# Clamps of weight words moved to VectorE, the causal mask of the maxima to TensorE, and new ranks in a planned attention and expert kernel

## The chip, the cores and the metric

The kernel runs on one core of one Trainium2 chip. Its engines work at the same time, each through its own queue of instructions in order: TensorE (PE; PEld is its weight load), VectorE (DVE), ScalarE (ACT), GpSimd (POOL), and SyncE (SP), which issues the DMAs. They wait for each other by semaphores. The metric is the device time of one execution in microseconds, lower is better.

## The reference

Inputs are float32 except where the weights come as float64, read as pairs of 32-bit words. Four batches, 8 heads, 576 positions, 64 columns a head:

```python
scores = scale * np.matmul(q, k.transpose(0, 1, 3, 2))
log_f = np.log(np.clip(f, 0.0001, 1.0))
cum = np.cumsum(log_f, axis=-1)
scores = np.where(causal, -1e9, scores + cum[:, :, :, None] - cum[:, :, None, :])
attn = softmax(scores)                 # with its row maximum subtracted
x = (attn @ v), heads side by side     # 2304 tokens x 512
x = (x @ w_a) * (x @ w_b) @ w_out      # 512 -> 1536 -> 512
h = x @ w_in                           # 512 -> 1024
solu = h * softmax(h)
out = layernorm(solu) * g_ln @ w_out2  # 1024 -> 512
```

## The kernel before

Products are made of parts: a float32 operand is split into a rounded high part (ScalarE casts it to the matmul's format) and the rest (a subtraction on VectorE or GpSimd), and three products high by high, low by high, high by low are added in PSUM.

**The stages.** Attention goes head by head. The first batch's heads are done twice, for their first 256 queries (kind K0) and for the rest (K1); those of the other three batches in one piece (KF). Per head: `turn` transposes k and q (line 752), `split_k` and `split_q` split them (763 to 784), `max_scores` multiplies once (806), takes each row's maximum with the causal mask added (819), transposes the maxima (828) and writes them as extra rows of q (840, 845); `scores` multiplies again with the maxima in (863 to 871), `exps` applies the exponential and splits it (913 to 937), `weigh` multiplies by v (969), `out_` divides (991 to 1023). `split_x` splits the result (1041 to 1046), and `up_unit` makes the up products (1059, 12 matmuls for w_a and 12 for w_b), multiplies the two (1080) and writes the result to DRAM (1084). There are 8 strips of tokens by 12 column tiles of such units. `down` reads it back and splits it (1292 to 1304) and makes the down products (1310, 12 matmuls a tile); `expert` does the second layer by tiles of 128 tokens: 1363, the softmax and norm (1378 to 1416), transposes (1425) and 1440.

**Weights.** `load_cols` turns a tile of doubles into float32 words: a DMA (592), then on ScalarE the high word's absolute value as a number (607) and three bits of the low word (611), a clamp to the range of exponents (616), two shifts and ors on VectorE (618, 622), for the last matrix a scale (627), ScalarE's cast (635) and the subtraction for the low part (640). There are 48 tiles of 512 columns and 8 of 256, so 56 clamps; 28 tiles are w_a and w_b, which the up products need.

**What sets the order.** Nothing is ordered by hand. Each operation is recorded with an engine (or several, the cheapest in the plan is taken), a rank `key`, a planned cost (`t_dve`, `t_pool1` and so on) and the parts of buffers it reads and writes. `Sched.run` then plays the operations through: on each engine, among those that can start within `WIN` of the first, the lowest rank goes first. Instructions are written out in that order, so a number in the table `Y` (ranks of the stages and weights, and choices) changes every queue. `fill` puts small bf16 products (1480), whose result nobody reads, on TensorE where the plan shows a gap of over 0.3 us before its 210 us; they keep TensorE busy and are real instructions in its queue.

Clamp and choice of engine, before:

```python
cl_ = op([("DVE", t_dve2(n)), ("POOL", t_pool1(n))][:Y["CL"]], key, None, ...)
cl_.fn = lambda: ENG[cl_.eng].tensor_scalar(
    out=wmv(), in0=wmv(), scalar1=W_MIN, scalar2=W_MAX, op0=ALU.max, op1=ALU.min)
```

With `CL` 2 the plan could choose, and put all 56 on GpSimd, whose planned cost was 0.67 us for 512 columns.

Of the kernel before, what the change touches and what calls it, by code (L numbers as in the profile page):

```python
# [276 lines left out]


Y = {
    "Z0": 10.901,  # L280
    "T0": 3.049,
    "T1": 5.81,
    "TA": 4.561,
    "TF": 20.444,
    "U0": 0.0,
    "U1": 1.931,
    "UF": 5.673,
    "UL": 5.395,
    "LEAD": (3.6808465587643813, 2.8668250590211586),
    "SHRINK": 0.372,  # L290
    "W0": 26.546,
    "WD0": 4.133,
    "WN": 4,
    "WD1": 0.984,
    "WD2": 2.48,
    "EZ": 15.392,
    "EO": 6.479,
    "TE": 15.456,
    "DL": 1,
    "BIAS": 0.302,  # L300
    "UO": (7.298276837196878, 10.587551391559384, 11.3464056171286),
    "UD": 48.049,
    "UK": 77.199,
    "L3": 6,
    "CL": 2,
    "TL": (0.0, 0.0),
    "F1": 210.0,
    "FG": 0.3,
    "FF": 0.7,
    "RA": 1,  # L310
    "MX": -2.229,
    "XK": -0.243,
    "WIN": 0.067,
}


# [1212 lines left out]
```

## Time and profile before

| | before |
|---|---|
| median of 3 runs | 976.86 us (975.46 to 980.66) |
| the profiled execution, its own time | 974.57 us |
| its span, first to last instruction | 972.8 us |
| TensorE busy | 930.5 us (96%), granted clock 0.988 |
| VectorE busy | 614.9 us (63%) |
| ScalarE busy | 462.5 us (48%) |
| GpSimd busy | 226.2 us (23%) |

The span is cut into stages below. The granted clock is a share of 2.4 GHz. "L616 POOL" in a row is line 616 on GpSimd; "out<-in" are the program's names of tiles (`wms`, `pfw`, `raws`, `xrw`, `nat` are buffers in which tiles are staged, `ps` is PSUM, `sets` the split k and q), and "<-ACT wms L607" is what ended the idle time before.

### The profile page before, as it was taken

Reading aid. Unit: us, or ns where it says so; the run is one execution under the profiler, and the core shown is the slowest. Engines: PE = TensorE matmul, PEld = TensorE weight load, DVE = VectorE, ACT = ScalarE, POOL = GpSimd, SP = SyncE. Lnnn points to the kernel's source line nnn. Section 1 sums busy time; section 2 is a strip of 40 time slices with the busy share of each in tenths; the row PEclk is TensorE's granted clock in tenths of the full one; section 3 lists DMA queues with packets and bytes.
Section 4 is the critical chain, followed back from the end, with each engine's and each line's share of the span. In section 5 each row is a group of like instructions: output and inputs, shape, how many; then the busy total and the mean of one; then the engine's idle time right before and its main releaser. Section 6 shows DMA issues by size and latency. Waiting matters only on the chain.

```text
span 972.8 us, 16051 instructions
## 1 busy us (share of the span) xinstructions
PE 930.5 (96%) x5878; PEld 842.9 (87%) x5878; DVE 614.9 (63%) x1207; ACT 462.5 (48%) x860; POOL 226.2 (23%) x277
## 2 busy tenths in 40 slices
PE   7888888899999999999999999999999999999997
PEld 5777877899999999999999987988888888888886
DVE  6787787777666767777663676644455554455554
ACT  4777666665664464655543564422232232232332
POOL 3265544334420220212232653300000000000000
PEclk9799999999999999999999999999999999999999
DMA  3655445333342332332334654411221212111000
GB/s 83 170 139 162 143 132 142 87 82 86 85 101 63 77 82 60 98 78 57 97 97 161 192 183 139 156 41 55 65 55 44 62 47 64 35 38 44 17 22 32
DMA packets 124002, 86.90 MB, mean 89 GB/s; under 512 B 74346, under 2 KB 114292, under 8 KB 123924
## 3 DMA queue, kind: packets, MB, share of 16 engines
q1 hardware_dynamic: 123924, 85.88, 31.7%
q8 instruction: 46, 0.75, 0.3%
q14 instruction: 32, 0.26, 0.1%
HBM read 56.86 MB, written 19.02 MB: 78 GB/s over the span
## 4 chain that ended last, share of the span: by engine, by line
PE 76%; DVE 7%; POOL 6%; ACT 5%; issue 3%; DMA 3%; SPq 1%; DVEq 0%; ACTq 0%; POOLq 0%
PE ps L1059 25%; PE ps L1310 14%; PE ps L1363 10%; PE ps L1440 9%; PE ps L969 7%; PE ps L871 3%; POOL pfw L616 2%; PE ps L806 2%; PE ps L863 2%; POOL wms L616 2%; PE ps L1425 2%; PE ps L752 1%; DVE wms L618 1%; DMA pfw<-in_moe_w_b_dram 1%; DVE wms L622 1%
## 5 line engine op out<-in xcount | busy, mean ns | idle before, releaser
L1059 PE MATMUL ps<-xs,wt 128*128 128x288 f32 (+2 forms) x2304 | 334.2, 299 | 4.9 <-DVE wt L640 3.8
L1059 PEld LDWEIGHTS ps<-xs,wt 128*128 128x128 f32 x2304 | 314.3, 189 | 8.8 <-DVE wt L640 5.0
L969 PE MATMUL ps<-pexp,VS 128*128 128x64 f32 (+5 forms) x600 | 98.4, 308 | 6.1 <-DVE pexp L935 3.5
L969 PEld LDWEIGHTS ps<-pexp,VS 128*128 128x128 f32 x600 | 93.4, 196 | 10.5 <-DVE pexp L935 4.3
L819 DVE CUSTOM_DVE_ANT_0 ps<-ps,cmask 64x576 f32<-64x576 f32 (+4 forms) x160 | 86.4, 551 | 20.0 <-PE ps L806 16.0
L1440 PE MATMUL ps<-wt 128*128 128x512 f32 x408 | 97.9, 389 | 0.0
L1310 PE MATMUL ps<-wt,sets 128*128 128x512 f32 (+1 forms) x420 | 95.3, 375 | 2.5 <-DVE wt L1302 2.5
L1440 PEld LDWEIGHTS ps<-wt 128*128 128x128 f32 x408 | 76.6, 188 | 15.9
L1310 PEld LDWEIGHTS ps<-wt,sets 128*128 128x128 f32 x420 | 73.2, 190 | 17.0 <-DVE wt L1302 4.3
L1078 ACT COPY ats<-ps 128x288 f32<-128x288 f32 (+2 forms) x96 | 38.0, 396 | 95.8 <-PE ps L1059 95.0
L922 POOL TENSOR_SCALAR_AFFINE_SELECT pfw<-pfw 128x128 f32<-128x128 f32 (+1 forms) x120 | 37.1, 338 | 185.7 <-ACT pfw L913 184.6
L1302 POOL TENSOR_TENSOR wt<-nat,wt 128x256 fp32r<-128x256 f32 (+1 forms) x9 | 8.9, 985 | 285.6 <-ACT wt L1298 285.6
L616 POOL TENSOR_SCALAR wms<-wms 128x512 f32<-128x512 f32 (+1 forms) x32 | 57.4, 1794 | 73.0 <-ACT wms L607 72.9
L1298 ACT CAST wt<-nat 128x512 fp32r<-128x512 f32 (+1 forms) x60 | 34.7, 578 | 83.4 <-PE ps L1310 74.1
L1302 DVE TENSOR_TENSOR wt<-nat,wt 128x512 fp32r<-128x512 f32 (+1 forms) x51 | 34.1, 668 | 61.6 <-ACT wt L1298 31.1
L1080 DVE TENSOR_TENSOR gts<-ps,ats 128x288 f32<-128x288 f32 (+2 forms) x84 | 38.1, 454 | 44.1 <-PE ps L1059 21.8
L1363 PE MATMUL ps<-wt 128*128 128x512 f32 x240 | 59.0, 395 | 0.7 <-DVE wt L1323 0.7
L616 POOL TENSOR_SCALAR pfw<-pfw 128x512 f32<-128x512 f32 x24 | 48.2, 2008 | 32.6 <-ACT pfw L607 32.5
L913 ACT ACTIVATE pfw<-ps 128x960 f32<-128x960 f32 (+1 forms) x48 | 38.6, 836 | 33.6 <-PE ps L871 33.4
L1363 PEld LDWEIGHTS ps<-wt 128*128 128x128 f32 x240 | 44.1, 188 | 9.8 <-DVE wt L1323 1.2
L863 PE MATMUL ps<-sets 128*128 128x64 f32 (+5 forms) x200 | 50.8, 299 | 1.8 <-DVE sets L840 1.0
L871 PE MATMUL ps<-sets 71*128 71x448 f32 (+4 forms) x200 | 51.9, 336 | 0.2
(158 smaller groups left out, 1506.4 us busy)
## 6 DMA issues: line engine op xcount, KB each, us to landing
gs<-gts SPq DMA_DIRECT2D x60, 144.0 KB
sets<-sets SPq DMA_DIRECT2D x56, 144.0 KB
nat<-gs SPq DMA_DIRECT2D x36, 144.0 KB
raws<-in_moe_w_a_dram SPq DMA_DIRECT2D x10, 512.0 KB
pfw<-in_moe_w_b_dram SPq DMA_DIRECT2D x10, 512.0 KB
nat<-gs SPq DMA_DIRECT2D x36, 128.0 KB
out_dram<-xrw SPq DMA_DIRECT2D x18, 256.0 KB
nat<-in_k_dram SPq DMA_DIRECT2D x32, 128.0 KB
```

The source lines that it names most:

```text
L616: cl_.fn = lambda: ENG[cl_.eng].tensor_scalar(out=wmv(), in0=wmv(), scalar1=W_MIN, scalar2=W_MAX, op0=ALU.max, op1=ALU.min)
L819: nc.vector.tensor_tensor_reduce(out=x, in0=x, in1=cmask[:n, off:off + w], scale=1.0, scalar=-3.0e38, op0=ALU.add, op1=ALU.max, accum_out= ...
L863: nc.tensor.matmul(dst, lhsT=SA(st)[:, ks], rhs=MA(st)[:, q0:q1], start=True, stop=False)
L871: nc.tensor.matmul(dst, lhsT=SB(st)[:D + NA, ks], rhs=MB(st)[:D + NA, q0:q1], start=False, stop=True)
L913: op(("ACT", t_act(n, True)), key + 5.5 + 0.9 * i, lambda i=i, n=n, pf=pf: nc.scalar.activation(out=pf(), in_=bank(ss[i], 0, n), func=AF.Exp),
L969: nc.tensor.matmul(bank(u, K.uo + q0, q1 - q0), lhsT=V[:, vp], rhs=src[:, o:o + q1 - q0], start=(k_ in K.first and ip == 0), stop=(k_ in K ...
L1059: nc.tensor.matmul(bank(u[m], 0, n_), lhsT=wv(m, wp, c)[:, kk], rhs=xsv(h, xx, n_)[:, kk], start=(n == 0), stop=(n == 3 * KD - 1))
L1080: op(("DVE", t_dve(n_)), key - 50.0, lambda: nc.vector.tensor_tensor(out=gtv(), in0=bank(u[1], 0, n_), in1=atv(), op=ALU.mult), r=[(u[1], ...
L1302: o.fn = lambda o=o, gr=gr, gb=gb: ENG[o.eng].tensor_tensor(out=ghv(gb, 1)[:, :n], in0=grv(gr)[:, :n], in1=ghv(gb, 0)[:, :n].bitcast(F32), ...
L1310: nc.tensor.matmul(bank(py, 512 * d, n), lhsT=WO[c][0][:, wp * DM:(wp + 1) * DM][:, ds_], rhs=ghv(gb, gp)[:, :n], start=(c == 0 and i == 0 ...
L1363: nc.tensor.matmul(bank(ph, half * 512, 512), lhsT=yv(yb, yp)[:, d, tsl], rhs=wi(d, wp)[:, fs], start=(n == 0), stop=(n == 3 * KD - 1))
L1440: nc.tensor.matmul(bank(po, 0, DM), lhsT=zp[:, c], rhs=w2(c, wp), start=(c == 0 and i == 0), stop=(c == NF2 - 1 and i == 2))
```

## The change

`CL` becomes 1: the clamp has only VectorE to choose. `MM` is new: for the first batch's heads (K0 and K1) `max_scores` adds the causal mask by a small product (identity by mask, 128 columns or 64) into the same bank of PSUM, and the maximum is a plain reduction instead of the custom add-and-maximum with its separate read of the accumulator. `TB` is new and 1, which leaves the three bits on ScalarE, as before. Three planned costs change (two of ScalarE's by 1.1, GpSimd's clamp, which is not chosen now). All other numbers of `Y` that change are ranks and the plan's weights. Lines behind the table stand a little lower in the new kernel: 616 becomes 627, 618 becomes 629, 640 becomes 651, 806 becomes 820, 819 becomes 839, 1059 becomes 1082, 1310 becomes 1333, 1480 becomes 1503; the mask's products are line 824.

```diff
-    "Z0": 10.901,
-    "T0": 3.049,
-    "T1": 5.81,
+    "Z0": 17.056,
+    "T0": 4.873,
+    "T1": 15.735,
...
-    "W0": 26.546,
-    "WD0": 4.133,
+    "W0": 0.0,
+    "WD0": 0.382,
...
-    "UD": 48.049,
-    "UK": 77.199,
+    "UD": 22.8,
+    "UK": 87.852,
     "L3": 6,
-    "CL": 2,
+    "CL": 1,
...
+    "TB": 1,
+    "MM": 1,
...
-        op(("ACT", t_act(n)), key - 0.6, lambda: nc.scalar.activation(
+        op(("ACT", t_act(1.1 * n)), key - 0.6, lambda: nc.scalar.activation(
...
-        cl_ = op([("DVE", t_dve2(n)), ("POOL", t_pool1(n))][:Y["CL"]], key, None, r=[(wm, 0)],
+        cl_ = op([("DVE", t_dve2(n)), ("POOL", 0.18 + n * 0.0034)][:Y["CL"]], key, None, r=[(wm, 0)],
...
             for o, w, i, k0 in K.mm[part]:
+                d0 = o + i * P - k0
+                dw = min(P, o + w - d0)
+                pm = K.pm and Y["MM"] and o <= d0 < o + w
                 nc.tensor.matmul(
                     bank(ms[part], o, w), lhsT=MB(st)[:D + 2, i * P:(i + 1) * P],
-                    rhs=SB(st)[:D + 2, k0:k0 + w], start=True, stop=True)
+                    rhs=SB(st)[:D + 2, k0:k0 + w], start=True, stop=not pm)
+                if pm:
+                    nc.tensor.matmul(
+                        bank(ms[part], d0, dw), lhsT=identb, rhs=cmask[:, 4 * P:4 * P + dw],
+                        start=False, stop=True)
...
+            if K.pm and Y["MM"]:
+                nc.vector.tensor_reduce(
+                    out=mt(st)[:n, 2 + i:3 + i], in_=x, op=ALU.max, axis=AX.X)
+                return
```

**VectorE in the first batch, a weight tile.** Before, between the last maxima of K0's heads and a K1 head's exponentials, the two word operations of one tile (618, 622) stand with no clamp; it is in GpSimd's queue.

```order
L1022 TENSOR_TENSOR xrw<-xrw 128x256
L618 SCALAR_TENSOR_TENSOR pfw<-pfw,raws 128x512
L935 TENSOR_TENSOR pexp<-ps,pexp 128x832
L1002 COPY xrw<-ps 64x256
L819 ISA ps,mts<-ps,cmask 64x576
L819 ISA mts 64x1
L622 SCALAR_TENSOR_TENSOR pfw<-raws,pfw 128x512
```

Now:

```order
L627 TENSOR_SCALAR wms<-wms 128x512
L1025 COPY xrw<-ps 64x256
L629 SCALAR_TENSOR_TENSOR wms<-wms,pfw 128x512
L977 TENSOR_TENSOR VS<-nat,VS 128x5x2x64
L633 SCALAR_TENSOR_TENSOR wms<-pfw,wms 128x512
L627 TENSOR_SCALAR pfw<-pfw 128x512
L839 TENSOR_REDUCE mts<-ps 128x1
L958 TENSOR_TENSOR pexp<-ps,pexp 128x832
L958 TENSOR_TENSOR pexp<-ps,pexp 128x384
L629 SCALAR_TENSOR_TENSOR pfw<-pfw,raws 128x512
```

The clamp (627) of each tile now stands in VectorE's own queue ahead of its word operations, and a maximum (839) is one instruction where it was two (819).

**TensorE around its last filler.** Before, the last filler (1480) is followed by the maxima and scores of the second batch's heads, and a head's products by v (969) lie ahead of it.

```order
L871 MATMUL ps<-sets 128x448
L1480 LDWEIGHTS identb
L1480 MATMUL ps<-cmask,identb 128x192
L1480 LDWEIGHTS identb
L1480 MATMUL ps<-cmask,identb 128x192
L1480 LDWEIGHTS identb
L1480 MATMUL ps<-cmask,identb 128x192
L806 MATMUL ps<-sets 128x512
L806 MATMUL ps<-sets 128x384
L806 MATMUL ps<-sets 128x128
L806 MATMUL ps<-sets 128x256 x2
L806 MATMUL ps<-sets 128x320
```

Now:

```order
L1503 LDWEIGHTS identb
L1503 MATMUL ps<-cmask,identb 128x192
L992 MATMUL ps<-pexp,VS 128x448 x6
L992 MATMUL ps<-pexp,VS 128x64 x3
L820 MATMUL ps<-sets 128x512
L820 MATMUL ps<-sets 128x384
L820 MATMUL ps<-sets 128x128
L992 MATMUL ps<-pexp,VS 128x320 x3
L992 MATMUL ps<-pexp,VS 128x192 x3
L992 MATMUL ps<-pexp,VS 128x128 x3
```

That head's 18 products by v now come behind the last filler. In all there are 406 fillers before and 376 now.

**TensorE at the start of the down products.** Before, behind the last head's products by v:

```order
L969 MATMUL ps<-pexp,VS 128x128 x3
L1059 MATMUL ps<-xs,wt 128x288 x492
L1310 MATMUL ps<-wt,sets 128x512 x12
L1059 MATMUL ps<-xs,wt 128x288 x24
L1310 MATMUL ps<-wt,sets 128x512 x12
```

Now:

```order
L992 MATMUL ps<-pexp,VS 128x128 x3
L1082 MATMUL ps<-xs,wt 128x288 x312
L1333 MATMUL ps<-wt,sets 128x512 x12
L1082 MATMUL ps<-xs,wt 128x288 x12
L1333 MATMUL ps<-wt,sets 128x512 x12
```

The first down product moves from behind 41 groups of 12 up products to behind 26; 69 groups in all stand behind the last head before, and 65 now.

## Rows read from the trace of the kernel before

**Rows 1.** View by stage; per engine busy us (instructions), then clock, DMA share, GB/s.
```profile
core 0: us, PE busy (x) PEld busy (x) DVE busy (x) ACT busy (x) POOL busy (x), PEclk, DMA share, GB/s
0.00:189.80 189.80, 157.10 (x1197) 139.62 (x1197) 145.48 (x302) 126.23 (x265) 87.09 (x98) 0.95 0.52 135
189.80:520.00 330.20, 329.18 (x2360) 321.46 (x2359) 226.39 (x457) 177.88 (x289) 79.58 (x145) 1.00 0.30 80
520.00:560.00 40.00, 40.00 (x294) 39.48 (x293) 23.90 (x38) 21.32 (x43) 21.27 (x12) 1.00 0.65 208
560.00:600.00 40.00, 37.47 (x195) 31.75 (x194) 29.64 (x46) 24.89 (x45) 20.75 (x11) 0.96 0.57 176
920.00:972.80 52.80, 47.54 (x234) 38.93 (x232) 27.33 (x61) 14.05 (x31) 0.54 (x1) 1.00 0.07 25
```

**Rows 2.** Groups by line on TensorE: busy us, mean ns; last, line 1480's own view.
```profile
L1059 PE MATMUL ps<-xs,wt 128*128 128x288 f32 (+2 forms) x2304 | 334.2, 299 | 4.9 <-DVE wt L640 3.8 <-DVE gts L1080 0.7 <-ACT ats L1078 0.4
...
L969 PE MATMUL ps<-pexp,VS 128*128 128x64 f32 (+5 forms) x600 | 98.4, 308 | 6.1 <-DVE pexp L935 3.5 <-DVE sets L768 2.2 <-POOL VS L954 0.3
...
L1480 PE MATMUL ps<-cmask,identb 128*128 128x192 bf16 x406 | 47.4, 264 | 0.6 <-DVE gts L1080 0.6
...
L867 PE MATMUL ps<-identb,cmask 128*128 128x128 bf16 (+1 forms) x40 | 9.3, 232 | 0.0
...
L1480 PE MATMUL ps<-cmask,identb x406: 242/246/383, 5.5 to 189.7; 128*128 128x192 bf16 x136
```

**Rows 3.** Chain of waits, 0 to 190 us: shares by line.
```profile
by line: POOL wms L616 7.8%; issue 7.5%; PE ps L969 5.3%; POOL pfw L616 5.2%; DMA pfw<-in_moe_w_b_dram 4.9%; PE ps L1059 4.1%; PE ps L1480 3.9%; DVE wms L618 3.5%; DVE wms L622 3.5%; POOL wt L640 3.2%; ACT wt L635 3.1%; PE ps L806 2.7%; SPq
```

**Rows 4.** Groups by line and shape on GpSimd, 0 to 190 us.
```profile
L616 POOL TENSOR_SCALAR pfw<-pfw 128x512 f32<-128x512 f32 x10 | 20.0, 1996 | 9.0 <-ACT pfw L607 8.9
L616 POOL TENSOR_SCALAR wms<-wms 128x256 f32<-128x256 f32 x8 | 9.0, 1129 | 8.3 <-ACT wms L607 8.3
```

**Rows 5.** Waits of VectorE, 0 to 190 us: us in total, times, longest.
```profile
DVE wms L618 <- POOL wms L616: 11.7, 11, 2.2
DVE pfw L618 <- POOL pfw L616: 8.6, 7, 2.3
```

**Rows 6.** Groups by line and shape on VectorE: tensor_scalar forms.
```profile
L627 DVE TENSOR_SCALAR wms<-wms,gln 128x512 f32<-128x512 f32 x4 | 2.2, 544 | 0.1
L627 DVE TENSOR_SCALAR pfw<-pfw,gln 128x512 f32<-128x512 f32 x4 | 1.9, 487 | 0.1
...
L530 DVE TENSOR_SCALAR xrw<-xrw 32x576 f32<-32x576 f32 x1 | 0.9, 912 | 0.0
...
L539 DVE TENSOR_SCALAR xs<-xrw 32x576 fp32r<-32x576 f32 x1 | 0.4, 448 | 0.0
```

**Rows 7.** The same view: maxima of 0 to 190 us, and a reduction of the whole run.
```profile
L819 DVE CUSTOM_DVE_ANT_0 ps<-ps,cmask 128x512 f32<-128x512 f32 x10 | 6.9, 687 | 0.8 <-PE ps L806 0.8
...
L819 DVE DVE_READ_ACCUMULATOR2_ANT mts<- 128x1 f32 x40 | 5.1, 126 | 0.2
...
L1378 DVE TENSOR_REDUCE sml<-ps 128x1 f32<-128x1024 f32 x18 | 22.0, 1224 | 27.8 <-PE ps L1363 27.8
```

**Rows 8.** The same view, 0 to 190 us: subtractions on VectorE, then on GpSimd.
```profile
L640 DVE TENSOR_TENSOR wt<-wms,wt 128x512 fp32r<-128x512 f32 x5 | 3.4, 686 | 0.0
...
L640 DVE TENSOR_TENSOR wt<-wms,wt 128x256 fp32r<-128x256 f32 x4 | 3.0, 750 | 0.0
...
L640 POOL TENSOR_TENSOR wt<-wms,wt 128x512 fp32r<-128x512 f32 x5 | 6.6, 1326 | 13.8 <-ACT wt L635 13.8
```

**Rows 9.** The same view, 0 to 190 us: lines 618 and 622 on VectorE.
```profile
L618 DVE SCALAR_TENSOR_TENSOR pfw<-pfw,raws 128x512 int32<-128x512 int32 x10 | 8.9, 892 | 8.7 <-POOL pfw L616 8.6
...
L622 DVE SCALAR_TENSOR_TENSOR pfw<-raws,pfw 128x512 int32<-128x512 int32 x10 | 7.8, 778 | 0.2
...
L618 DVE SCALAR_TENSOR_TENSOR wms<-wms,pfw 128x512 int32<-128x512 int32 x10 | 6.9, 688 | 8.5 <-POOL wms L616 8.5
```

**Rows 10.** Chain of waits, 555 to 640 us: shares by line.
```profile
by line: PE ps L1059 40.0%; PE ps L1310 20.4%; POOL pfw L616 9.5%; issue 4.1%; DMA nat<-gs 3.9%; DVE wt L1302 3.6%; ACT pfw L607 3.3%; POOL wms L616 2.9%; DVE wt L640 2.5%; DVE pfw L622 1.9%; ACT wt L635 1.5%; DVE pexp L640 1.4%; PE ps L136
```

**Rows 11.** Order of time on TensorE in the down stage: start, us, what.
```profile
560.65 2.93 PE L1310 MATMUL ps<-wt,sets 128*128 128x512 f32 x12
```

More of the change, by code (lines that the diff above doesn't have):

```diff
@@ L279 @@
 Y = {
-    "Z0": 10.901,
-    "T0": 3.049,
-    "T1": 5.81,
[L283 to L290, printed above, removed]
-    "W0": 26.546,
-    "WD0": 4.133,
-    "WN": 4,
[L294 to L298, printed above, removed]
+    "Z0": 17.056,
+    "T0": 4.873,
+    "T1": 15.735,
+    "TA": 4.417,
+    "TF": 21.695,
+    "U0": 8.749,
+    "U1": 0.0,
+    "UF": 6.93,
+    "UL": 1.453,
+    "LEAD": (1.3559648255683812, 1.1661755750630942),
+    "SHRINK": 1.832,
+    "W0": 0.0,
+    "WD0": 0.382,
+    "WN": 4,
+    "WD1": 4.394,
+    "WD2": 4.294,
+    "EZ": 11.965,
+    "EO": 25.007,
+    "TE": 17.338,
     "DL": 1,
-    "BIAS": 0.302,
-    "UO": (7.298276837196878, 10.587551391559384, 11.3464056171286),
-    "UD": 48.049,
-    "UK": 77.199,
+    "BIAS": 0.48,
+    "UO": (8.320466715924777, 16.68815323789424, 17.92095945373172),
+    "UD": 22.8,
+    "UK": 87.852,
     "L3": 6,
-    "CL": 2,
+    "CL": 1,
     "TL": (0.0, 0.0),
@@ L310 @@
     "RA": 1,
-    "MX": -2.229,
-    "XK": -0.243,
-    "WIN": 0.067,
+    "TB": 1,
+    "MM": 1,
+    "MX": -0.17,
+    "XK": -0.753,
+    "WIN": 0.02,
 }
@@ L604, in load_cols, with three @@
            after=CUM if kind == 0 else after)
-        op(("ACT", t_act(n)), key - 0.6, lambda: nc.scalar.activation(
+        op(("ACT", t_act(1.1 * n)), key - 0.6, lambda: nc.scalar.activation(
             out=wmv(), in_=hi_w().bitcast(F32), func=AF.Abs, scale=65536.0),
            r=[(raw, 0)], w=[(wm, 0)])
-        op(("ACT", t_act(n)), key - 0.5, lambda: nc.scalar.activation(
-            out=lo_w(), in_=low_byte(), func=AF.Copy, scale=1.0 / 32, bias=-31.0 / 64),
-           r=[(raw, 0)], w=[(raw, 1)])
-        cl_ = op([("DVE", t_dve2(n)), ("POOL", t_pool1(n))][:Y["CL"]], key, None, r=[(wm, 0)],
+        tb = op([("ACT", t_act(1.1 * n)), ("DVE", t_dve(n))][:Y["TB"]], key - 0.5, None,
+                r=[(raw, 0)], w=[(raw, 1)], port=True)
+        def three():
+            if tb.eng == "ACT":
+                nc.scalar.activation(
+                    out=lo_w(), in_=low_byte(), func=AF.Copy, scale=1.0 / 32, bias=-31.0 / 64)
+            else:
+                nc.vector.tensor_scalar(
+                    out=lo_w(), in0=lo_w(), scalar1=29, scalar2=None, op0=ALU.logical_shift_right)
+        tb.fn = three
+        cl_ = op([("DVE", t_dve2(n)), ("POOL", 0.18 + n * 0.0034)][:Y["CL"]], key, None, r=[(wm, 0)],
                  w=[(wm, 0)], port=True)
@@ L805, in mm @@
             for o, w, i, k0 in K.mm[part]:
+                d0 = o + i * P - k0
+                dw = min(P, o + w - d0)
+                pm = K.pm and Y["MM"] and o <= d0 < o + w
                 nc.tensor.matmul(
                     bank(ms[part], o, w), lhsT=MB(st)[:D + 2, i * P:(i + 1) * P],
-                    rhs=SB(st)[:D + 2, k0:k0 + w], start=True, stop=True)
+                    rhs=SB(st)[:D + 2, k0:k0 + w], start=True, stop=not pm)
[3 more added lines that the diff above has]
+                        start=False, stop=True)
         for part in range(len(K.mm)):
-            op((PE, t_mm([x[1] for x in K.mm[part]])), key + 0.1 * part, lambda part=part: mm(part),
-               r=[(st, "kh"), (st, "qh"), (st, "cum0"), (st, "cum1"), (st, "rows")],
+            more = [P for x in K.mm[part] if K.pm and Y["MM"] and x[3] <= x[2] * P < x[3] + x[1]]
+            op((PE, t_mm([x[1] for x in K.mm[part]] + more)), key + 0.1 * part,
+               lambda part=part: mm(part), r=[(CONST, "cmask"), (CONST, "identb"), (st, "kh"), (st, "qh"), (st, "cum0"), (st, "cum1"), (st, "rows")],
                w=[(ms[part], i) for _, _, i, _ in K.mm[part]])
@@ L823, in max_scores @@
         for j, (part, o, w, i) in enumerate(K.red):
-            op(("DVE", t_dve(w) + 0.14), key + Y["MX"] + 0.3 + 0.3 * j,
+            op(("DVE", t_dve(w) + (0.0 if K.pm and Y["MM"] else 0.14)), key + Y["MX"] + 0.3 + 0.3 * j,
                lambda part=part, o=o, w=w, i=i: red(part, o, w, i),
```

## Prediction

> **What bounds the kernel now.** I read the table by stage first. From 190 us on TensorE is busy for 329.2 of 330.2 us, then for 40 of 40 and 37.5 of 40, and only the last 53 us hold another 5.3 us of idle time [rows 1]. Its work there is the same in both kernels (the same 2304 products by w_a and w_b, 600 by the values, and so on), so moving it about costs or gives nothing unless a gap opens. The front is different: in the first 189.8 us TensorE is busy for 157.1 us, and of that 47.4 us are the 406 filler products that only keep it busy [rows 1, 2]; the last of them starts at 189.7 us [rows 2]. So 32.7 us idle and 47.4 us of filler, 80 us together, is what can be won, and nearly all of it lies there.
>
> What holds the front back is the chain of waits in it: 13.0% of it (7.8% and 5.2% of 190 us, 24.7 us) is GpSimd's clamp, line 616, more than any other line [rows 3]. One clamp of 512 columns takes 2.0 us, one of 256 takes 1.13 us [rows 4]; 28 of the 56 lie in the front. VectorE, busy for 145.5 of 189.8 us [rows 1], stands idle for 20.3 us (11.7 and 8.6) because its next instruction, line 618, waits for a clamp [rows 5]. As VectorE takes its instructions in order, everything queued behind waits too: the maxima, the splits of k and q, the low parts of the weights, and through them TensorE.
>
> **The change, part by part.** I cut both programs at TensorE's last filler and counted what stands ahead of it.
>
> *Clamps.* 28 leave GpSimd and 28 join VectorE. Nothing before shows this clamp on VectorE; the nearest row is line 627, a tensor_scalar of the same 128x512 tile, at 487 and 544 ns, and from below line 539's 448 ns on 576 columns of fewer partitions [rows 6]. I take 0.49 us, since line 627 has the shape, and 0.3 us for 256 columns (an estimate, between half of that and all of it). On VectorE that adds 20 x 0.49 + 8 x 0.3 = 12.2 us of work. On the chain of the front 13 pieces of clamp, 24.7 us together, become 13 x 0.49 = 6.4 us: **18.3 us shorter**.
>
> *Other work on VectorE ahead of the cut.* The first batch's maxima become a plain reduction: 40 separate reads of the accumulator go, 40 x 0.126 = 5.0 us [rows 7]. The reduction itself I take as long as the custom operation (687 ns for 512 columns; a reduction of 1024 takes 1224 ns, so 0.61 us at the least). The new ranks give GpSimd more of the subtractions: 6 of line 640 (2 x 0.7 + 4 x 0.75 us), and of lines 954, 1022, 1045 and 1002 another 7 (one of them goes to ScalarE), in all 7.8 us off VectorE [rows 8]; 2.4 us are only put off behind the cut. The slower of its two-input operations, which run beside clamps (ten of line 618 at 892 ns against 688, ten of line 622 at 778 [rows 9]), should lose 10 x 0.20 + 10 x 0.09 = 2.9 us. Sum: 145.5 + 12.2 - 5.0 - 7.8 - 2.4 - 2.9 = 139.6 us.
>
> *Where the front then ends.* Lower bound: VectorE's idle time shrinks by all of its waits for clamps, 44.3 - 20.3 = 24.0 us, and 139.6 + 24.0 = 163.6 us. Upper bound: other waits take their place and it stays busy for the same 76.7%, 139.6/0.767 = 182.0 us. The chain gives 189.8 - 18.3 = 171.5 us, near the middle of the two, and I take it: **18.3 us earlier**. GpSimd then has 87.1 - 49.4 + 10.3 = 48 us of work (the 10.3 us are the subtractions that come to it, at its own durations, as 1.3 us for one of line 640 [rows 8]) in 171 us.
>
> *What is put off.* At its last filler the new order has done 12 products of line 1059 (new: 1082) and 18 of line 969 (new: 992) fewer; at their means of 0.146 and 0.164 us [rows 2] that is 4.7 us, to be paid later on a full TensorE.
>
> *The mask on TensorE.* 40 small products are added, 0.23 us each by line 867's row [rows 2], 9.2 us. All are ahead of the cut, where 80 us of TensorE's time is idle or filler, so I take nothing; without that cover they would cost 9.2 us. The 30 fillers fewer (406 to 376) are 3.5 us of no value.
>
> *The middle and the end.* The down products begin after 26 groups of 12 up products behind the last head instead of 41. TensorE does the same work, so I take nothing; the cover is weights that arrive in time, priced in the rivals. The last 28 clamps lie here, where the chain of waits also passes through line 616 (12.4% of 555 to 640 us [rows 10]), so 560 to 600 us may lose its 2.5 us of idle time: within the range. The last tiles' order is the same from the last eight transposes on, and its 5.3 us stay.
>
> Sum: 974.57 - 18.3 + 4.7 = 961.0 us for the profiled execution. That execution is 2.29 us under the median of the three runs, 976.86; against the median **963.3 us**.
>
> **A rule that speaks against it.** Two rows of the same 32x576 tensor_scalar on VectorE differ twofold, 912 and 448 ns [rows 6]; the slow one lies at 4 us, where GpSimd fills its constants. The Trainium skill (SBUF — State Buffer, Who interferes with whom) says why: VectorE's fast modes and GpSimd share a pair of ports under an exclusive lock, and the later one waits for the whole instruction. By that rule a clamp on VectorE may have to wait for a subtraction on GpSimd; the trace agrees as far as those two rows go. By the rows alone the sum is the 963.3 us above; with the wait in full it is rival 1.
>
> **The rivals.**
> 1. *The waits only change their name.* Clamps now stand in VectorE's own queue, and GpSimd's longer subtractions (1.3 us for line 640 [rows 8]) stop them. With GpSimd busy for 48 of 171 us and half of 1.3 us to wait, the mean is 0.18 us, 5 us over 28 clamps, which leaves the gain. If every clamp waits 0.65 us more, 18.2 us, the front ends where it did, and with the 4.7 us put off the median is 981.5 us; at half of that it is 972.4 us, no change. For it: the 912 ns. Against: GpSimd loses 49.4 us of instructions that stopped VectorE just so. No change: 0.15.
> 2. *The down stage starves, slower.* Between the first load of a down weight into xrw and the last down product of the first block, the new order issues 14 weight tiles of 0.52 MB, 12 of 0.26 MB of products read back and 8 writes of 0.15 MB, 11.6 MB, while TensorE does 15.7 groups of 1.74 us and 11 of 2.9 us [rows 2, 11]: 59 us, 197 GB/s. The queues moved 208 GB/s from 520 to 560 us and 176 from 560 to 600 [rows 1]. At 176 they are 7 us late and the kernel is still faster; from about 150 GB/s (77 us, 18 us late) it decides. At 140 GB/s they take 83 us, 24 us too long: 963.3 + 24 = 987 us. Against: before, the like stretch (20 tiles, 15.9 MB) took some 84 us at 188 GB/s with only 2.5 us of idle time. 0.07.
> 3. *Little is done by the move*, because the front is bound by ScalarE (126 of 189.8 us [rows 1]; its casts and the top three bits stay there): the front ends at 182 us, the median is 973.8 us. This is the upper bound above, counted in the forecast's range.
>
> **How the numbers follow.** Forecast, front 8 to 26 us shorter: 0.78. The ends are 976.86 - 26.2 + 4.7 = 955.4 and 976.86 - 7.8 + 4.7 = 973.8 us; an us or so either way in the down stage or at the mask makes 954 and 975. That leaves out the far part of rival 1, rival 2 and a little below, some 2 in 10. Range 954 to 975. 0.5% is 4.9 us, about what a measurement of this kernel can tell from no change: faster than 972.0 us 0.77, within 0.16, slower than 981.7 us 0.07.
>
> **What would show it.** In the changed profile: the last filler at 165 to 180 us; clamps on VectorE at 0.45 to 0.55 us; no wait of line 629 (618 before) for GpSimd; GpSimd at some 45 to 50 us in that stretch; TensorE idle for at most 1% between there and 520 us. It is wrong if the last filler stays past 183 us, if clamps on VectorE show 0.8 us or more, or if the down stage holds over 8 us of idle TensorE.

## The result and the profile after

| | before | after |
|---|---|---|
| median on the same chip | 976.16 us (975.31 to 980.66) | 952.25 us (949.74 to 952.64) |
| the profiled execution, its own time | 974.57 us | 949.74 us |
| its span | 972.8 us | 947.7 us |
| last filler starts at | 189.7 us | 166.5 us |
| span behind the last filler | 783.1 us | 781.2 us |

The ratio is 0.974, interval 0.9706 to 0.9775: 2.6% faster, some 24 us where 13.6 us were forecast. The time lies just below the range. Two more measurements of the changed kernel on other chips follow (runs 17 and 18 below): 953.11 us at 0.978 and 952.08 us at 0.9766, some 21 and 23 us faster than the kernel before there. The profiled execution of the changed kernel is the shortest of its four; the others took 952.03 to 952.64 us.

The page of the changed kernel: busy time by engine, and the engines' shares of the chain that ended last.

```profile
PE 916.3 (97%) x5888; PEld 835.8 (88%) x5888; DVE 598.1 (63%) x1162; ACT 460.2 (49%) x862; POOL 189.3 (20%) x280
...
PE 81%; DVE 2%; ACT 1%; issue 0%; POOL 0%; DVEq 0%; ACTq 0%
```

The chain is TensorE's for 81% of the span (76% before); GpSimd, 6% of it before, has rounded to nothing. Where the time went is read from the table by stage. For the changed kernel, with its own last filler as the first border:

```profile
core 0: us, PE busy (x) PEld busy (x) DVE busy (x) ACT busy (x) POOL busy (x), PEclk, DMA share, GB/s
0.00:166.50 166.50, 142.67 (x1176) 129.43 (x1176) 141.60 (x272) 124.26 (x264) 49.08 (x81) 0.97 0.57 149
166.50:500.00 333.50, 332.16 (x2392) 325.89 (x2390) 223.73 (x446) 179.62 (x292) 98.90 (x161) 1.00 0.31 81
500.00:540.00 40.00, 40.00 (x256) 37.33 (x254) 28.53 (x51) 24.92 (x48) 4.42 (x5) 1.00 0.68 230
540.00:580.00 40.00, 40.00 (x247) 36.89 (x246) 23.88 (x41) 19.85 (x37) 3.01 (x2) 1.00 0.49 155
580.00:610.00 30.00, 30.00 (x228) 30.00 (x227) 23.87 (x42) 15.52 (x30) 4.75 (x4) 1.00 0.49 151
610.00:640.00 30.00, 29.27 (x141) 24.24 (x140) 16.06 (x30) 9.96 (x19) 5.27 (x5) 1.00 0.16 45
```

and the kernel before, where the down stage and the second layer begin:

```profile
500.00:540.00 40.00, 40.00 (x302) 40.00 (x301) 16.36 (x27) 14.14 (x30) 10.63 (x6) 1.00 0.45 148
540.00:580.00 40.00, 39.23 (x247) 35.58 (x245) 29.26 (x46) 25.17 (x46) 24.72 (x13) 1.00 0.56 174
580.00:610.00 30.00, 28.23 (x146) 24.57 (x147) 21.17 (x35) 14.76 (x27) 10.74 (x6) 0.94 0.46 143
610.00:640.00 30.00, 29.27 (x208) 28.30 (x207) 16.10 (x28) 12.77 (x25) 7.82 (x4) 1.00 0.41 137
```

The front answers to [rows 1]: 166.5 us instead of 189.8, with VectorE busy for 141.6 us and GpSimd for 49. From there to 610 us TensorE stands idle for 1.3 us of 443.5. The new thing is 540 to 610 us: before, TensorE lost 2.5 us there and was granted 0.94 of its clock in the second part; now it loses nothing at full clock. Which work that touched shows in TensorE's groups, after:

```profile
L1082 PE MATMUL ps<-xs,wt 128*128 128x288 f32 (+2 forms) x2304 | 332.0, 298 | 0.6 <-ACT ats L1101 0.5 <-DVE gts L1103 0.2
...
L992 PE MATMUL ps<-pexp,VS 128*128 128x64 f32 (+5 forms) x600 | 96.8, 303 | 6.4 <-ACT pexp L952 3.3 <-DVE pexp L958 2.1 <-ACT pfw L936 0.8
L1333 PE MATMUL ps<-wt,sets 128*128 128x512 f32 (+1 forms) x420 | 92.7, 370 | 0.0
```

the last filler's own view, after:

```profile
L1503 PE MATMUL ps<-cmask,identb x376: 243/246/368, 5.9 to 166.5; 128*128 128x192 bf16 x188
```

and one group of before that the forecast did not show:

```profile
L1310 PE MATMUL ps<-wt,sets 128*128 128x512 f32 (+1 forms) x420 | 95.3, 375 | 2.5 <-DVE wt L1302 2.5
```

Against [rows 2], lines 1082 and 992 answer to 1059 and 969. The down products of line 1333 took 92.7 us where they took 95.3, and their 2.5 us of waiting for VectorE's split of `wt` are gone.

VectorE's front, by its waits and by line and shape:

```profile
DVE pfw L627 <- ACT pfw L609: 9.2, 3, 4.5
...
DVE pfw L629 <- ACT raws L618: 0.9, 1, 0.9
```

```profile
L629 DVE SCALAR_TENSOR_TENSOR pfw<-pfw,raws 128x512 int32<-128x512 int32 x10 | 7.1, 709 | 1.1 <-ACT raws L618 0.9
...
L839 DVE TENSOR_REDUCE mts<-ps 128x1 f32<-128x512 f32 x8 | 5.5, 686 | 0.3 <-PE ps L824 0.2
L627 DVE TENSOR_SCALAR wms<-wms 128x512 f32<-128x512 f32 x10 | 5.3, 527 | 0.5 <-ACT wms L609 0.5
L627 DVE TENSOR_SCALAR pfw<-pfw 128x512 f32<-128x512 f32 x10 | 5.1, 513 | 9.2 <-ACT pfw L609 9.2
...
L627 DVE TENSOR_SCALAR wms<-wms 128x256 f32<-128x256 f32 x8 | 3.3, 416 | 0.1
```

The waits for GpSimd's clamps [rows 5] are gone; the longest wait left is that of three clamps for ScalarE. Lines 629 and 633 lost their slow cases [rows 9]: 709 ns where 892 stood, and 700 where 778 stood. A reduction of 512 columns takes what the custom operation took [rows 7], 686 ns beside 687.

### The profile page after: what moved, and what is told of

Same layout as the page of the kernel before. It is cut to its first block, busy times and chain, and to the rows that moved or that the text cites. A ratio compares the mean times of both kernels' runs of the same rounds, so it can differ in the third digit from the quotient of the medians.

```text
span 947.7 us, 16069 instructions
## 1 busy us (share of the span) xinstructions
PE 916.3 (97%) x5888; PEld 835.8 (88%) x5888; DVE 598.1 (63%) x1162; ACT 460.2 (49%) x862; POOL 189.3 (20%) x280
## 4 chain that ended last, share of the span: by engine, by line
PE 81%; DVE 2%; ACT 1%; issue 0%; POOL 0%; DVEq 0%; ACTq 0%
PE ps L1082 29%; PE ps L1333 16%; PE ps L1386 10%; PE ps L1463 10%; PE ps L992 7%; PE ps L894 2%; PE ps L820 2%; PE ps L886 2%; PE ps L1448 2%; PE ps L763 1%; DVE ps L842 0%; PE ps L851 0%; ACT pfw L936 0%; ACT pexp L952 0%; DVE wms L629 0%
## 5 line engine op out<-in xcount | busy, mean ns | idle before, releaser
L992 PEld LDWEIGHTS ps<-pexp,VS 128*128 128x128 f32 x600 | 90.5, 189 | 11.5 <-DVE pexp L958 3.5
L1333 PE MATMUL ps<-wt,sets 128*128 128x512 f32 (+1 forms) x420 | 92.7, 370 | 0.0
L1325 POOL TENSOR_TENSOR wt<-nat,wt 128x512 fp32r<-128x512 f32 (+1 forms) x26 | 27.4, 1054 | 251.1 <-ACT wt L1321 251.1
L842 DVE CUSTOM_DVE_ANT_0 ps<-ps,cmask 128x512 f32<-128x512 f32 (+4 forms) x120 | 64.6, 551 | 11.5 <-PE ps L820 8.6
L1403 ACT ACTIVATE xrw<-ps,sml 128x1024 f32<-128x1024 f32 x17 | 19.0, 1118 | 79.3 <-DVE sml L1401 79.3
L1454 DVE TENSOR_TENSOR wt<-ps,wt 128x512 fp32r<-128x512 f32 x34 | 23.3, 689 | 53.3 <-ACT wt L1451 53.3
L1401 DVE TENSOR_REDUCE sml<-ps 128x1 f32<-128x1024 f32 x18 | 22.0, 1225 | 49.2 <-PE ps L1386 49.2
L958 DVE TENSOR_TENSOR pexp<-pfw,pexp 128x960 fp32r<-128x960 f32 (+1 forms) x40 | 41.2, 1042 | 14.9 <-ACT pexp L952 14.8
```

What stands on the lines that cost most here:

```text
L842: nc.vector.tensor_tensor_reduce(out=x, in0=x, in1=cmask[:n, off:off + w], scale=1.0, scalar=-3.0e38, op0=ALU.add, op1=ALU.max, accum_out= ...
L958: o.fn = lambda o=o, bh=bh, bl=bl, n=n, pf=pf: ENG[o.eng].tensor_tensor(out=pexp[:, 64 * bl.slot:64 * bl.slot + n], in0=pf(), in1=pexp[:, ...
L992: nc.tensor.matmul(bank(u, K.uo + q0, q1 - q0), lhsT=V[:, vp], rhs=src[:, o:o + q1 - q0], start=(k_ in K.first and ip == 0), stop=(k_ in K ...
L1333: nc.tensor.matmul(bank(py, 512 * d, n), lhsT=WO[c][0][:, wp * DM:(wp + 1) * DM][:, ds_], rhs=ghv(gb, gp)[:, :n], start=(c == 0 and i == 0 ...
```

## The experiments

Each is measured beside runs of the kernel before on the same chip. Most changes of a number make the planner write a new order, so the first nine test a part with the order that the plan then gives; the nine behind them hold the order fixed and change only what is issued.

### Parts with a new plan

**1. Clamps alone, old ranks** (on the kernel before).

```diff
-    "CL": 2,
+    "CL": 1,
```

> The kernel before with one number changed: the clamps have only VectorE to choose, old ranks, no mask products. Theory 'clamp' (the clamp's engine makes the gain, whatever the ranks): 956 to 963 us, the last filler at 167 to 176 us, no wait of line 618 for a clamp. Rival 'ranks' (the order found for the new costs makes most of it): 967 to 974 us. Rival 'mask': 970 to 976 us.

962.60 us, ratio 0.9876 (0.9861 to 0.9891), last filler at 180.2 us. About half of the gain comes without one new rank.

**2. Ranks alone**: the new table in the kernel before, the clamp held on GpSimd at its old planned cost.

```diff
-        cl_ = op([("DVE", t_dve2(n)), ("POOL", t_pool1(n))][:Y["CL"]], key, None, r=[(wm, 0)],
+        cl_ = op([("DVE", t_dve2(n)), ("POOL", t_pool1(n))][1:2], key, None, r=[(wm, 0)],
```

> The kernel before with the new table of ranks and weights alone; all clamps on GpSimd at the old planned cost, no mask products. Theory 'clamp': 970 to 982 us, VectorE waits 15 us or more for clamps in the front. Rival 'ranks': 955 to 964 us.

977.84 us, ratio 1.0026 (1.0012 to 1.004), last filler at 179.1 us. The front is 10.6 us shorter and the kernel is no faster: what the front won was lost behind it.

**3. The changed kernel without the mask's part.**

```diff
-    "MM": 1,
+    "MM": 0,
```

> The changed kernel without the mask products: maxima of the first batch by the custom operation and its read of the accumulator again. 40 reads at 0.126 us are 5 us of VectorE in a front where VectorE is busy for 85%. Theory 'clamp': 952 to 957 us. Rival 'mask' (the part that was priced too low): 958 us or more.

958.61 us, ratio 0.9829 (0.9814 to 0.9843). Read alone this says that the mask is worth 6 us. Its plan has 463 fillers instead of 376, though, so this is another order, and runs 14 and 16 contradict it.

**4. The changed kernel with its clamps on GpSimd**, planned at their true cost.

```diff
-        cl_ = op([("DVE", t_dve2(n)), ("POOL", 0.18 + n * 0.0034)][:Y["CL"]], key, None, r=[(wm, 0)],
+        cl_ = op([("DVE", t_dve2(n)), ("POOL", 0.18 + n * 0.0034)][1:2], key, None, r=[(wm, 0)],
```

> The changed kernel with all 56 clamps on GpSimd, which the plan now takes at 1.92 us. Theory 'clamp': 966 us or more, the last filler past 180 us. Rival 'ranks': under 960 us. A plan that knows the true cost but keeps the engine would land between, 960 to 966 us.

964.55 us, ratio 0.9897 (0.988 to 0.9913), last filler at 181.3 us. With the new ranks, the mask's part and a plan that knows how slow GpSimd's clamp is, the kernel is 1% faster than before and 1.2 to 1.6% behind the changed kernel. The same operations in the changed kernel's own order (run 11) gain 0.2%.

**5. Clamps and mask, old ranks**: the changed code with the table of the kernel before, in which only these numbers differ:

```diff
-    "CL": 2,
+    "CL": 1,
+    "TB": 1,
+    "MM": 1,
```

> The old table of ranks with both other parts: clamps on VectorE and the mask products. If the parts add (clamp alone -12.5 us, products -6.4 us): 955 to 958 us, so that the new ranks are worth 4 to 6 us. If the products help only in the new order: 961 to 963 us.

960.49 us, ratio 0.9852 (0.9834 to 0.9871): beside run 1 (0.9876) hardly better.

**6. Only the planned cost of GpSimd's clamp corrected**, in the kernel before.

```diff
-        cl_ = op([("DVE", t_dve2(n)), ("POOL", t_pool1(n))][:Y["CL"]], key, None, r=[(wm, 0)],
+        cl_ = op([("DVE", t_dve2(n)), ("POOL", 0.18 + n * 0.0034)][1:2], key, None, r=[(wm, 0)],
```

> The kernel before with nothing but the planned cost of GpSimd's clamp put right (1.92 us for 512 columns); old ranks, clamps still on GpSimd. Theory 'plan' (a good part of what the clamp cost before was a plan that took it for 0.67 us and queued work behind it): 964 to 971 us. Rival 'engine': 973 us or more.

989.03 us, ratio 1.0143 (1.0108 to 1.0178): slower, with the last filler at 191.6 us. A truer cost with ranks that were chosen for the false one gave a worse order than the false one had given.

**7. Old ranks of the weights** in the changed kernel.

```diff
-    "W0": 0.0,
-    "WD0": 0.382,
+    "W0": 26.546,
+    "WD0": 4.133,
...
-    "WD1": 4.394,
+    "WD1": 0.984,
```

> The changed kernel with the three old numbers that rank the w_a and w_b tiles (W0, WD0, WD1), so that their preparation starts late again (first clamp at some 32 us instead of 17). Theory 'early weights' (the new order gains because the weights' preparation fills VectorE in the first 60 us): the front 5 us or more longer, 956 to 966 us. Rival (other ranks do it): 950 to 954 us.

961.44 us, ratio 0.9867 (0.9848 to 0.9887), last filler at 169.6 us.

**8. New ranks of the weights** in run 5's kernel.

```diff
-    "W0": 26.546,
-    "WD0": 4.133,
+    "W0": 0.0,
+    "WD0": 0.382,
...
-    "WD1": 0.984,
+    "WD1": 4.394,
```

> Old ranks, clamps on VectorE and mask products, with only the three new numbers that rank the w_a and w_b tiles. Theory 'early weights': 953 to 957 us, most of the way from the old ranks (0.985 of before) to the changed kernel (0.974). Rival: no better than the old ranks, 959 us or more, since the other ranks are made for late weights.

1002.73 us, ratio 1.029 (1.0266 to 1.0313), last filler at 198.2 us. The ranks that serve the new table ruin the old one; no number of the table has a price of its own.

**9. A number that should mean nothing**, in the changed kernel.

```diff
-    "WIN": 0.02,
+    "WIN": 0.03,
```

> The changed kernel with one number that means nothing for the engines, the plan's window, at 0.03 instead of 0.02 us: every part of the change is in it, in another order (400 fillers instead of 376). If the new table is a fit to one order, as the runs with other weights' ranks and without the products suggest: 955 to 962 us. If its ranks are good in themselves: 950 to 954 us.

958.80 us, ratio 0.984 (0.981 to 0.9871). Some 6 us are lost by this one step beside the fitted order; no other such step was tried. A part's price read from a new plan can carry an error of that size, so runs 1 to 8 price nothing finer.

### Parts at a fixed order

**10. The old order, its clamps issued on VectorE** (plan untouched).

```diff
-        cl_.fn = lambda: ENG[cl_.eng].tensor_scalar(
+        cl_.fn = lambda: nc.vector.tensor_scalar(
```

> The kernel before in exactly its own order (the plan still takes the clamps for GpSimd's), but the 56 clamps are issued on VectorE. This is the forecast's term alone, the chain's -18.3 us, nothing re-planned. Theory 'clamp' (the engine gives it in any order): 957 to 964 us, about what the re-planned old ranks gave (0.988). Rival 'order' (the gain needs a plan that knows where the clamps are): 967 us or more.

959.62 us, ratio 0.9839 (0.9816 to 0.9863), 15.7 us of 974.42. The span is 957.3 us with the last filler at 179.2: 10.5 us in the front, 5.0 us behind it. Stages, then the group of line 1310:

```profile
540.00:580.00 40.00, 40.00 (x234) 36.09 (x233) 34.44 (x63) 26.29 (x47) 0.00 (x0) 1.00 0.64 192
580.00:610.00 30.00, 30.00 (x194) 28.09 (x193) 19.45 (x37) 14.57 (x27) 0.00 (x0) 1.00 0.50 151
```

```profile
L1310 PE MATMUL ps<-wt,sets 128*128 128x512 f32 (+1 forms) x420 | 93.0, 371 | 0.0
```

The 2.5 us of idle time and the reduced clock of 540 to 610 us are gone, and the down products are at 371 ns, without a wait. Nothing else changed, so moving the clamps was worth 5 us behind the front.

**11. The new order, its clamps issued on GpSimd.**

```diff
-        cl_.fn = lambda: ENG[cl_.eng].tensor_scalar(
+        cl_.fn = lambda: nc.gpsimd.tensor_scalar(
```

> The changed kernel in exactly its own order, but the 56 clamps are issued on GpSimd, each at its place in time. Theory 'clamp': +12 us or more over the changed kernel, 964 to 975 us, with VectorE's waits for clamps back at 15 to 20 us in the front.

972.78 us, ratio 0.9978 (0.9961 to 0.9996). The span is 967.2 us with the last filler at 175.0: 792.2 us lie behind it, 11.0 more than in the changed kernel. Its stages:

```profile
500.00:540.00 40.00, 38.27 (x261) 36.44 (x260) 16.74 (x27) 16.82 (x34) 15.62 (x11) 1.00 0.51 176
540.00:580.00 40.00, 36.67 (x193) 31.60 (x192) 27.20 (x42) 21.46 (x39) 18.24 (x10) 0.96 0.46 139
580.00:610.00 30.00, 30.00 (x219) 29.52 (x218) 16.34 (x25) 13.24 (x26) 15.69 (x9) 1.00 0.52 162
610.00:640.00 30.00, 26.97 (x169) 24.87 (x169) 19.21 (x30) 12.34 (x24) 11.59 (x7) 0.94 0.35 106
```

its chain of waits from 520 to 640 us, by line:

```profile
by line: PE ps L1082 17.3%; POOL wms L627 13.6%; issue 11.9%; PE ps L1333 11.4%; POOL pfw L627 8.9%; DVE pfw L629 5.8%; PE ps L1386 5.5%; DMA pfw<-in_moe_w_out_dram 3.7%; ACT wms L609 3.6%; DVE wms L629 3.3%; DVE pfw L633 3.1%; DVE wms L633
```

that of the changed kernel over the same stretch:

```profile
by line: PE ps L1082 52.0%; PE ps L1333 36.4%; PE ps L1386 9.0%; PE ps L1463 1.1%; PE ps L1448 0.7%; DVE wt L1346 0.5%; DVE gts L1103 0.4%; issue 0.1%; DVEq L1103 0.0%
```

its down products, and VectorE's waits in its front:

```profile
L1333 PE MATMUL ps<-wt,sets 128*128 128x512 f32 (+1 forms) x420 | 93.3, 371 | 2.1 <-DVE wt L1325 2.1
...
L1333 PE MATMUL ps<-wt,VS 128*128 128x512 f32 (+1 forms) x120 | 28.6, 389 | 3.0 <-DVE wt L1325 3.0
```

```profile
DVE pfw L629 <- POOL pfw L627: 8.5, 5, 4.3
DVE wms L629 <- POOL wms L627: 7.5, 7, 2.0
```

GpSimd's clamp is 22.5% of this chain (13.6 and 8.9) and absent from the changed kernel's. TensorE is idle for 8.1 us between 500 and 640 us, against 0.7 with the clamps on VectorE.

**12. The new order with all of the old operations**: the diffs of runs 11, 14 and 15 together.

> The new order alone, exactly, with the operations of before: clamps on GpSimd, no mask products, the custom maxima. If the order is worth the 8 to 10 us that the forecast left out: 962 to 967 us. If the new order has its worth only with the clamps on VectorE: 972 us or more.

972.51 us, ratio 0.9968 (0.9951 to 0.9986), last filler at 176.5 us, 792.0 us behind it. So the order alone is worth some 3 us: 13.2 us won in the front, 8.9 us lost behind it, of which 4.7 us are products that it puts off.

**13. Each clamp twice**, in the changed kernel's order.

```diff
-        cl_.fn = lambda: ENG[cl_.eng].tensor_scalar(
-            out=wmv(), in0=wmv(), scalar1=W_MIN, scalar2=W_MAX, op0=ALU.max, op1=ALU.min)
+        cl_.fn = lambda: [ENG[cl_.eng].tensor_scalar(
+            out=wmv(), in0=wmv(), scalar1=W_MIN, scalar2=W_MAX, op0=ALU.max, op1=ALU.min)
+            for _ in range(2)]
```

> The changed kernel, same order, with every clamp done twice on VectorE: 20 x 0.42 + 8 x 0.28 = 10.6 us more work in the front. If VectorE bounds the front, as 85% busy says: +8 to +12 us, 960 to 964 us. If it has slack there: +2 to +5 us.

956.87 us, ratio 0.9817 (0.9795 to 0.9838). 28 more clamps in the front, at the changed kernel's medians of 0.42 and 0.28 us some 10.6 us of VectorE's time, cost 4 to 5 us beside run 14 of the same chip: VectorE sets the front's end only in part. The 28 behind the front cost nothing: the last filler starts at 172.1 us, and 781.1 us lie behind it.

**14. Mask's products kept, maxima by the custom operation**, fixed order.

```diff
-            if K.pm and Y["MM"]:
-                nc.vector.tensor_reduce(
-                    out=mt(st)[:n, 2 + i:3 + i], in_=x, op=ALU.max, axis=AX.X)
-                return
```

> The changed kernel, same order, with the mask products kept and the custom operation with its read of the accumulator back on VectorE (the mask is added twice, which leaves the maxima as they are). If the products' 6.4 us come from VectorE's shorter maxima: 956 to 960 us. If they come from the order that the plan makes of them: 952 to 954 us.

952.39 us, ratio 0.9768 (0.9746 to 0.979): as the changed kernel. The 40 reads of the accumulator, 5.0 us of VectorE's time, are worth nothing that can be measured.

**15. Mask's products left out, plain maxima**, fixed order.

```diff
-                pm = K.pm and Y["MM"] and o <= d0 < o + w
+                pm = False
```

> The changed kernel, same order, without the 40 mask products: the maxima of the first batch are then over masked columns too. If the products are hidden by TensorE's idle time, as forecast: within 1.5 us of the changed kernel. If they are paid at 0.23 us each: 4 to 9 us less.

949.13 us, ratio 0.974 (0.972 to 0.9759), last filler at 163.2 us. The maxima are then taken over masked columns too. Beside run 17 of the same chip this is 4 us better, with intervals that lie just apart (run 17's begins at 0.9762).

**16. Neither products nor plain maxima**: the diffs of 14 and 15 together, so this is the changed kernel's order with the clamps as its only new operation.

> The changed kernel's own order with the clamps on VectorE, but the 40 mask products left out and the 40 maxima by the custom add-and-maximum as before, so the whole computation stands. If the products are what the mask's move costs (4 us by the run without them) and the custom operation is as long as the reduction, 949 us, ratio 0.974, with the last filler at 163 to 168 us. If the 40 separate reads of the accumulator (5 us of VectorE's time) matter again once nothing hides them, 952 to 954 us, 0.978.

951.82 us, ratio 0.9751 (0.9728 to 0.9774), last filler at 170.7 us. Beside run 18 of the same chip (0.9766) the medians show no difference: by them the whole move of the mask is worth nothing.

**17 and 18. The changed kernel again**, on the chips of runs 7, 8 and 15, and of run 16.

> The changed kernel itself once more, on the chip of the three below: 0.974 of the kernel before, 949 to 952 us. It is the measure for them.

> The changed kernel once more, beside the run before it on the same chip, as its measure: 952 to 953 us, ratio 0.976 to 0.978, last filler at 166 to 171 us.

953.11 us, ratio 0.978 (0.9762 to 0.9798), and 952.08 us, ratio 0.9766 (0.9748 to 0.9784). The last filler starts at 171.0 and 169.2 us; behind it lie 781.2 and 781.3 us, as in the first profile.

## Why the prediction was wrong

The fixed orders, by the profiled executions, cut at the last filler:

| order | clamps on | mask's part | front, us | behind, us | span, us |
|---|---|---|---|---|---|
| old (before) | GpSimd | no | 189.7 | 783.1 | 972.8 |
| old (run 10) | VectorE | no | 179.2 | 778.1 | 957.3 |
| new (run 12) | GpSimd | no | 176.5 | 792.0 | 968.5 |
| new (run 11) | GpSimd | yes | 175.0 | 792.2 | 967.2 |
| new (run 16) | VectorE | no | 170.7 | 781.1 | 951.8 |
| new (after, 17, 18) | VectorE | yes | 166.5, 171.0, 169.2 | 781.2, 781.2, 781.3 | 947.7, 952.2, 950.5 |

**The step that failed** is "*The middle and the end*", with its "so I take nothing". The sum had 4.7 us more behind the last filler; it came out 1.8 to 1.9 us less, in each of three profiles. The 4.7 us are there: line 1082's 12 products and line 992's 18 that are put off show as 4.2 us more of these two lines behind the cut. Against them stand the last clamps, for which the down stage waited before. Its longest idle time, in order of time on three engines:

```profile
582.70 2.31 POOL L616 TENSOR_SCALAR pfw<-pfw 128x512 f32<-128x512 f32 x1 [2.01 <-ACT pfw L607]
...
585.05 0.69 DVE L618 SCALAR_TENSOR_TENSOR pfw<-pfw,xrw 128x512 int32<-128x512 int32 x1 [1.81 <-POOL pfw L616]
585.66 0.69 DVE L1302 TENSOR_TENSOR wt<-nat,wt 128x512 fp32r<-128x512 f32 x1
...
586.39 3.71 PE L1310 MATMUL ps<-wt,sets 128*128 128x512 f32 x10 [1.77 <-DVE wt L1302]
```

A clamp keeps VectorE's line 618 waiting for 1.81 us, the split of `wt` for a down product stands behind it in VectorE's queue, and TensorE stands idle for 1.77 us. With the clamps on VectorE there is 2.5 us less idle time (0.7 instead of 3.3 from 500 to 640 us) and 2.6 us less on line 1333's products, which before ran at a granted clock of 0.94 behind the idle time. Together that is 5.1 us, and run 10 shows 5.0 us by moving the clamps alone. The last 1.0 us is spread over other lines. In the new order the same clamps on GpSimd would have cost 11.0 us (run 11). The forecast had the evidence: 12.4% of 85 us of the chain [rows 10] is 10.5 us of clamp, priced there as at most 2.5 us of idle time "within the range". Of the 11 us by which the profiled execution undercut its sum, 6.6 lie behind the last filler and the rest in the front; in runs 17 and 18 the front undercut its term by only 0.4 and 2.2 us.

**The front's 18.3 us** came out as 23.2, 18.7 and 20.5 us, so the term was near, but partly by luck, since its origin was not as told. In the old order the clamps alone shorten the front by 10.5 us (run 10), not by the 18.3 us that stood in the chain: VectorE's idle time there falls from 44.3 to 29.5 us and not by all of its 20.3 us of waits, and its work grows by 4.2 us. The order alone shortens the front by 13.2 us (run 12), but little of that is a gain of its own: 4.7 us are products put off, and 4.2 us more are lost behind the front while the clamps are on GpSimd. By the ratios the clamp's engine is worth 15.7 us in the old order (run 10) and 1.98 to 2.12% in the new one (run 11 against 17 and 18), 19 to 21 us; the order is worth 3 us with GpSimd's clamps (run 12) and, together with the mask's part, 6 to 7 us with VectorE's (0.9839 against 0.978 and 0.9766). Each seems to make the other worth more.

**Clamps on VectorE** were taken as 12.2 us of work in the front; the rows add up to 13.7. The median of one is 419 to 423 ns for 512 columns (GpSimd: 1.92 us), and the mean 0.52, inside the forecast's 0.45 to 0.55. Six of the 28 account for the difference. Order of time, both engines:

```profile
38.75 1.29 POOL L651 TENSOR_TENSOR wt<-pfw,wt 128x512 fp32r<-128x512 f32 x1 [3.27 <-ACT wt L646]
...
39.28 1.04 DVE L627 TENSOR_SCALAR wms<-wms 128x512 f32<-128x512 f32 x1 [0.47 <-ACT wms L609]
...
113.55 0.41 DVE L627 TENSOR_SCALAR wms<-wms 128x512 f32<-128x512 f32 x1
...
113.70 1.00 POOL L1045 TENSOR_TENSOR xrw<-xrw 128x320 f32<-128x320 f32 x1 [0.43 <-DVE xrw L1039]
...
117.66 0.95 POOL L1068 TENSOR_TENSOR xs<-xrw,xs 128x320 fp32r<-128x320 f32 x1 [2.96 <-ACT xs L1064]
...
117.78 1.11 DVE L627 TENSOR_SCALAR pfw<-pfw 128x512 f32<-128x512 f32 x1
```

The clamp at 39.28 us began while GpSimd's subtraction ran (38.75 to 40.04) and ended 0.28 us behind it, at 40.32; that at 117.78 began behind one that ran to 118.61 and ended at 118.89. The one at 113.55 began first and took its 0.41 us. All six that took 0.65 us or more began, like the first two, during one of GpSimd's two-input operations, and no other did; over 0.42 us (0.28 for 256 columns) they cost 3.1 us together. That is rival 1's mechanism at a price of 3 us, where it needed 18 to take the gain; the forecast's 0.49 us for one clamp happened to hold 1.6 us of it (12.2 us of work against 10.6 at these medians). The Trainium skill (SBUF — State Buffer, Who interferes with whom) says that the engine that comes second waits for the other's whole instruction; these rows agree.

**The mask** was taken as 5.0 us off VectorE and nothing on TensorE. By the medians of runs 16 and 18 the whole move changes nothing. The products may still cost some 3 us: run 15, without them, is 4 us faster than run 17, and run 16, also without them, agrees with it where executions of like granted clock are compared. At a mean clock of 0.993, runs 15 and 16 took 948.26 and 947.92 us and run 18 took 951.26 to 952.49; at 0.989 they took 950.42 and 950.09 us and run 17 took 951.88 to 954.29. Three of run 16's five executions were granted less than 0.989, and its median is one of them. The forecast took the products as hidden in idle time and fillers; with so few executions their price is not settled.

**VectorE's work in the front** is 141.6 us for 139.6 forecast, GpSimd's 49 for 48, TensorE's idle time from there to 520 us 1.3 us: as told, in sum. The lower bound, that VectorE's waits for clamps vanish and none replaces them, gave 163.6 us; its idle time is now 24.9 us where that bound had 24.0, so the first profile's 166.5 us is this bound nearly.

**Rival 2** (the down stage starves) did not come with the change, though its place is right: it is what run 11 shows, by the clamps and not by the transfers. **Rival 3** would have put the front's end at 182 us; it came at 166.5 to 171.0.

What stays open: which of the ranks carry the new order (runs 7 and 8 show that they work only together), why orders beside the fitted one lost 6 us or more (runs 7 and 9), and what the mask's products cost. The fronts and what lies behind them come from one profile of each kernel, and from three of the changed one.

## What to carry to other kernels

A helper operation that moves is priced in every stage whose chain of waits it stands in, not only where its share is greatest: here 5 of 16 us (old order) and 11 of some 20 (new order) lay in the second place. Where a planner writes the order, a part is tested with the order held and only the issued instruction changed, since a new plan alone moved the time by 6 us for a number without meaning. And an order fitted to one set of costs is fitted again when a cost changes: correcting a false cost alone made the kernel 1.4% slower.

## What was not expected of the hardware

The front's length in the same program goes with the clock that TensorE was granted in it, and a weight tile that lands late can stand at the start of that. The first profile of the changed kernel and that of run 17, 40 to 50 us:

```profile
40.00:50.00 10.00, 7.14 (x69) 6.04 (x66) 9.09 (x20) 9.03 (x24) 2.60 (x4) 1.00 0.59 160
```

```profile
40.00:50.00 10.00, 6.28 (x47) 5.71 (x48) 7.81 (x17) 7.50 (x20) 2.57 (x3) 0.77 0.49 138
```

Up to 40 us the two are alike; here run 17 is granted 0.77 where the first was granted 1.00. What stands ahead of it, in run 17:

```profile
44.61 0.66 ACT L609 ACTIVATE pfw<-raws 128x512 f32<-128x512 f32 x1 [2.02 <-DMA raws<-in_moe_w_a_dram]
...
46.10 0.38 PE L851 MATMUL ps<-ident,mts 128*7 128x128 f32 x1 [3.15 <-DVE mts L839]
```

ScalarE waited 2.02 us for the load of a weight tile, in the first profile 0.73. The tile's clamp then held VectorE's queue for 1.98 us (0.70), the maximum behind it came late, and TensorE stood idle for 3.15 us (1.87). From 46 to 50 us it was granted 0.50. So a clamp in VectorE's queue passes a late transfer on to TensorE, which the forecast did not price. The last filler starts 4.5 us later, and behind it both profiles need 781.2 us.

In the first 60 us ScalarE's three waits for these loads add up to 7.0, 9.1 and 8.0 us in the three profiles of the changed kernel, the mean granted clock is 0.91, 0.89 and 0.86, and the fronts end at 166.5, 169.2 and 171.0 us. The shortest front has the shortest waits; the other two are ordered by the clock and not by the waits. In run 16 the clock is 0.83 there and in run 15 it is 0.94, which may be why the medians of these two disagree about the products.

In run 8 TensorE stands idle for 3.63 us before 213.2 us, waiting for a maximum, and is granted 0.50 from 214 to 236 us. Over 20 us no other run shows so low a clock (0.67 in run 16 is the next):

```profile
200.00:220.00 20.00, 15.85 (x76) 14.96 (x77) 15.31 (x34) 9.40 (x17) 1.27 (x5) 0.73 0.33 91
220.00:240.00 20.00, 18.25 (x71) 16.57 (x72) 12.46 (x27) 12.34 (x22) 4.72 (x10) 0.51 0.38 88
```

A group of the second stretch by shape, and the same over the whole of run 8:

```profile
L1082 PE MATMUL ps<-xs,wt 128*128 128x256 f32 x12 | 2.8, 415 | 0.0
```

```profile
L1082 PE MATMUL ps<-xs,wt 128*128 128x256 f32 x288 | 42.6, 300 | 1.8 <-DVE wt L651 1.1 <-POOL wt L651 0.4 <-ACT wt L646 0.3
```

TensorE counts as busy for 18.25 of 20 us at a granted 0.51, nearly all of it at the lower of the clock's two levels, 1.2 GHz; products of the same shape take 415 ns where their mean over the run is 300. A busy share near full hides such a loss; the clock's column and the time of one product show it.
